# A gated mix of a state-space scan and an FFN: first loads by DMA transposes, and another order of the products

## The chip, the cores and the metric

The kernel runs on one core of a Trainium2 chip. The metric is the device time of one execution in microseconds. Before the change it is 143.59 us, the median of three runs (142.94 to 143.62).

A core has five engines with a queue of instructions each: TensorE (PE, matmuls; PEld is its weight load), VectorE (DVE), ScalarE (ACT), GpSimd (POOL) and SyncE (SP, which here only issues DMAs). Each works through its own queue in order. They wait for each other by semaphores.

## The reference

```python
x = A_x                                               # 2048 tokens x 448
g = sigmoid((x * gate_w).sum(-1, keepdims=True))
# A: a diagonal complex state-space layer, 448 states
Lam_bar = exp(exp(log_dt) * Lam)                      # Lam = Lambda_re + i Lambda_im
Bu = x @ (((Lam_bar - 1) / Lam)[:, None] * Bmat).T    # complex
h[t] = Lam_bar * h[t-1] + Bu[t]
a = 2 * real(h @ Cmat.T) + x * Dskip
# B: a dense FFN, 448 -> 1792 -> 448
b = silu(x @ w1) @ w2
out = g * a + (1 - g) * b
```

Inputs and output are bfloat16.

## The kernel before

**Products.** The 2048 tokens are worked in four chunks of 512 (`CH`). For each chunk there are seven tiles of Bu (`bu(tc, s)`: 448 real and 448 imaginary states, as 7 x 128) and fourteen tiles of the first FFN layer (`f1(tc, fb)`). Both are products over the 448 features with the transposed x (`xT`). 448 is three and a half times 128, so two tiles are always made together as a pair, on the upper and lower 64 rows of PE at once. `step` (L605) opens a pair with eight matmuls of 64 rows and closes the pair before it with six (`half_steps`, L596; `close`, L621). All of these matmuls have line L599. `BU(tc, (a, b))` and `F1(tc, (a, b))` write out such pairs. The second layer is `ffn2(tb)` (`F2`, L697): fourteen matmuls (L703) for 128 tokens. The readout of the states is `readout(tb)` (`C`, L717): seven matmuls (L731) for 128 tokens, and then VectorE's combination with the gate and x (L721, L735) and the store.

**Results and their banks.** The products land in eight banks of PSUM; a pair takes two. A bank is used again when its result has been taken out: an FFN tile by ScalarE with SiLU (L692, into `aT`), a Bu tile by ScalarE (L633) or, for four tiles of the first chunk, by VectorE (L631), into `U`. There is one `U` for all chunks, so a tile of the next chunk can be written there only after `lanes` of the chunk before has read it. A second-layer block leaves by ScalarE (L707, into `Tb`).

**The recurrence.** `lanes(tc)` (L654) turns `U` by cosines and sines (L652: products into `PA` and `PB`, and their sum), so that the complex recurrence becomes seven real scans (L665, into `Gf`). Each scan's result is converted to bfloat16 (`Gb`) by ScalarE (L671) or by GpSimd (L669); the table `GP` (L626) says which ones go to GpSimd. Then `Gb` is turned back into `H` (L652). Slot 3 is half real and half imaginary, and its halves are exchanged by two small DMAs (`swapped`).

**Parameters.** The four vectors come by ScalarE's DMA queue, are transposed by PE (L487, L489) and copied into `pc` (L495). From `pc` follow the cosine and sine tables on VectorE, ScalarE and GpSimd (L501 to L548), then `s8` and `c8` (L557, L559), and from these a chain of about twenty GpSimd operations on a few columns (`pt`, L562 and L565 to L589) to `SS`, `CC`, `sc1` and `sc2`. `readout_weights(k)` (L741) scales the transposed C with `sc2` on ScalarE (L757, L759, into `ct`) and with `sc1` on VectorE (L761, L764, into `CP`).

**Loads.** SP issues, in this order: x's first chunk as it is (`xnat`), B in four loads, w1 in ten, w2, x's second chunk by transposing DMAs (`load_xt`, L370), C by two transposing DMAs (L389) and three small loads. PE transposes x's first chunk (`x_transposes`, L437) and all of B (`b_transposes`, L459), and VectorE and ScalarE copy them out (L447, L449, L475, L477). `idle(n)` (L420) lets PE multiply zeros, n times 256 columns (L425).

**What sets the order.** `Plan` (L47) is a list scheduler that runs on the host when the program is built. PE's order is the order in which the code adds the products, written out at L800 to L868. On the other engines it picks, of the instructions that could start first by the plan's own costs, the one with the lowest `prio`. A cost is written at each instruction (0.10 to 0.15 us for the small GpSimd operations, `act_cost` and `dve_cost` for the rest). The result is a fixed order for each queue, with fixed waits.

Of the kernel before, what the change touches and what calls it, by code (L numbers as in the profile page):

```python
# [8 lines left out]
AF = mybir.ActivationFunctionType  # L9
# [252 lines left out]
def bass_gated_mix__ssm_conv_s5__dense_activation_silu__prompt_kernel(nc, A_x, A_Lambda_re, A_Lambda_im, A_B_re, A_B_im, A_C_re, A_C_im,  # L262
               A_log_dt, A_Dskip, B_x, B_w1, B_w2, gate_w, out):
    with ExitStack() as ctx:
# [24 lines left out]
        Bnat = Tb[:, 0:7, :]  # L289
# [67 lines left out]


# [7 lines left out]
        def load_xt(tc, n, prio, cost, reads=()):  # L366

            rows = slice(tc * CH, (tc + n) * CH)
            for k, (o, c) in enumerate(((slice(0, 3), slice(0, 384)), (slice(3, 4), slice(320, 448)))):
                P.add("sp", lambda e, o=o, c=c: e.dma_start_transpose(xT[:, o, rows], x2[rows, c]), list(reads),  # L370
                      [f"xT{t}{k}" for t in range(tc, tc + n)], cost[k], prio + k, sem(), n * CH * (1100, 500)[k])

        load_x(0, 0)
        load("sp", Bnat[:, 0:3, :], A_B_re[0:384, :].rearrange("(s p) d -> p s d", p=128), "Bn0", 384 * 896, 1)
        load("sp", Bnat[:, 4:7, :], A_B_im[0:384, :].rearrange("(s p) d -> p s d", p=128), "Bn3", 384 * 896, 2)
        load("sp", Bnat[0:64, 3, :], A_B_re[384:448, :], "Bn1", 64 * 896, 3)
        load("sp", Bnat[64:128, 3, :], A_B_im[384:448, :], "Bn2", 64 * 896, 4)
        for h, (c0, c1) in enumerate(((0, 384), (384, 896))):
            w = w1s[:, :, :].rearrange("p b (q f) -> p b q f", q=2)
            for b in range(3):  # L380
                load("sp", w[:, b, :, c0:c1], B_w1[128 * b:128 * b + 128, :].rearrange("p (q f) -> p q f", q=2)[:, :, c0:c1],
                     f"w1{h}{b}", 128 * 4 * (c1 - c0), 5 + h)
            load("sp", w[64:128, 3, :, c0:c1], B_w1[384:448, :].rearrange("p (q f) -> p q f", q=2)[:, :, c0:c1],
                 f"w1{h}3", 64 * 4 * (c1 - c0), 5 + h)
            load("sp", w1s[0:64, 3, c0:c1], B_w1[320:384, c0:c1], f"w1{h}4", 64 * 2 * (c1 - c0), 5 + h)
# [11 lines left out]
        def late_loads():  # L397
            load_xt(2, 2, 16, (6.0, 1.4), ["Gb7a", "Gb7b"])
            load("sp", dsk[:, :],
                 A_Dskip.rearrange("(o n) -> o n", o=1).partition_broadcast(128).rearrange("p o n -> p (o n)"),  # L400
                 "dsk", 128 * 896, 18, ["Gb7b"])
            for tc in range(1, NCH):
                load_x(tc, 18 + tc, ["Gb7b"])
# [11 lines left out]
        ACT(lambda e: e.preload_act_table(AF.Exp), [], ["tbl"], 1.3, 4)  # L415


        DVE(lambda e: e.memset(PB[:, 0, :], 0.0), [], ["PB0"], 0.2, 0)  # L418
# [10 lines left out]
        idle(15)  # L429


        def x_transposes(h, n):

            tk = Ps()

            def mm(pe):
                for q in range(2):  # L437
                    for b in range(2):
                        o = (q * 2 + b) * 128
                        c = XCOL[2 * n + q]  # L440
                        r = pe.transpose(bk16(tk)[:, o:o + 128], xnat[:, 2 * h + b, c:c + 128], ident[:, :])  # L441
                return r
            P.add("pe", mm, ["xn0", "ident"], [tk], 0.24)
            dst = xT[:, 2 * n:2 * n + 2, 256 * h:256 * h + 256]
            src = lambda: bk16(tk)[:, 0:512].rearrange("p (q n) -> p q n", q=2)
            if n == 0:
                DVE(lambda e: e.tensor_copy(dst, src()), [tk], [f"xT00{h}"], 0.42, 0)  # L447
            else:
                ACT(lambda e: e.activation(dst, src(), AF.Copy), [tk], [f"xT01{h}"], act_cost(512), 0)  # L449

        for h in range(2):
            for n in range(2):
                x_transposes(h, n)

        def xr(tc):
            return [f"xT{tc}{k}" for k in (range(2) if tc else ("00", "01", "10", "11"))]

        def b_transposes(slots, reads, h, to_act):

            tk = Ps()  # L460
            n = len(slots)

            def mm(pe):
                for q in range(2):
                    i = 2 * h + q
                    for j, s in enumerate(slots):
                        o = (q * n + j) * 128
                        r = pe.transpose(bk16(tk)[:, o:o + 128], Bnat[:, s, XCOL[i]:XCOL[i] + 128], ident[:, :])  # L468
                return r
            P.add("pe", mm, reads + ["ident"], [tk], 0.06 * 2 * n)  # L470
            dst = BT[:, 2 * h:2 * h + 2, slots[0] * 128:(slots[-1] + 1) * 128]
            src = lambda: bk16(tk)[:, 0:2 * n * 128].rearrange("p (q m) -> p q m", q=2)
            name = f"BT{h}_{slots[0]}"
            if to_act:
                ACT(lambda e: e.activation(dst, src(), AF.Copy), [tk], [name], act_cost(256 * n), 0)  # L475
            else:
                DVE(lambda e: e.tensor_copy(dst, src()), [tk], [name], 0.1 + 0.00058 * 256 * n, 0)  # L477

        B01, B23, B456 = (0, 1), (2, 3), (4, 5, 6)
        b01, b23, b456 = ([f"BT{h}_{s}" for h in range(2)] for s in (0, 2, 4))  # L480
# [11 lines left out]
        b_transposes(B01, ["Bn0"], 0, False)  # L492
        b_transposes(B01, ["Bn0"], 1, True)
        idle(2)
# [96 lines left out]

        def half_steps(pe, a, b, lo, hi, start):  # L596
            for i in range(len(lo)):
                for p0, (w, xc, tk, c0), k in ((0, a, lo[i]), (64, b, hi[i])):
                    r = pe.matmul(bk(tk), w[p0:p0 + 64, k, c0:c0 + 128], xT[p0:p0 + 64, k, xc:xc + CH],  # L599
                                  start=(start and i == 0), stop=(not start and i == 2))  # L600
            return r

        open_pair = []

        def step(ta, tb):  # L605

            (wa, xa, ca, ra, ea), (wb, xb, cb, rb, eb) = ta, tb
            a, b = Ps("pair"), Ps("pair")
            begin = lambda pe: half_steps(pe, (wa, xa, a, ca), (wb, xb, b, cb), (0, 1, 2, 3), (0, 1, 2, 3), True)
            end = lambda pe: half_steps(pe, (wb, xb, b, cb), (wa, xa, a, ca), (0, 1, 2), (0, 1, 3), False)  # L610
            reads = ra + rb

            def evict(a, b):
                ea(a)
                eb(b)
            P.add("pe", begin, reads, [a, b], 0.866, rows=64)
            if open_pair:
                close()
            open_pair.append((end, reads, a, b, evict))

        def close():  # L621
            end0, reads0, a0, b0, evict0 = open_pair.pop()
            P.add("pe", end0, reads0, [], 0.65, acc=[a0, b0], rows=64)
            evict0(a0, b0)

        GP = ((), (0, 1), (0, 1), ())  # L626


        def u_out(s, tk, on_dve=False):
            if on_dve:  # L630
                DVE(lambda e: e.tensor_copy(U[:, s, :], bk(tk)), [tk], [f"U{s}"], dve_cost(512), 2)  # L631
            else:
                ACT(lambda e: e.activation(U[:, s, :], bk(tk), AF.Copy), [tk], [f"U{s}"], act_cost(512), 4)  # L633

        def bu(tc, s):
            def evict(tk):
                u_out(s, tk, tc == 0 and s in (1, 2, 5, 6))
                if s == 3 and tc:
                    swapped(U, "U", 0)
                elif s == 3:  # L640
                    for k, p in ((0, 0), (1, 64)):
                        DVE(lambda e, p=p: e.tensor_copy(U[p:p + 64, 7, :], U[64 - p:128 - p, 3, :]),
                            ["U3"], [f"U7{'ab'[k]}"], dve_cost(512, 4), 2)
            return BT, CH * tc, 128 * s, xr(tc) + (b01, b01, b23, b23, b456, b456, b456)[s], evict

        def swapped(t, tn, prio):
            for k, (p, q) in enumerate(((0, 64), (64, 0))):
                P.add("sp", lambda e, p=p, q=q: e.dma_start(t[p:p + 64, 7, :], t[q:q + 64, 3, :]),
                      [f"{tn}3"], [f"{tn}7{'ab'[k]}"], 0.55, prio, sem(), 65536)
# [4 lines left out]
        def lanes(tc):  # L654
# [7 lines left out]
            for s in (3, 0, 4, 1, 5, 2, 6):  # L662
# [7 lines left out]
                else:  # L670
                    ACT(lambda e, s=s: e.activation(Gb[:, s, :], Gf[:, s, :], AF.Copy), [f"Gf{s}"], [f"Gb{s}"], act_cost(512), 4)  # L671
# [18 lines left out]
        def f1(tc, fb):  # L690
# [3 lines left out]
            part = 0 if fb % 7 < 3 else 1  # L694
            return w1s, CH * tc, 128 * fb, xr(tc) + [f"w1{part}{n}" for n in range(5)], evict

        def ffn2(tb):  # L697
# [3 lines left out]
            def mm(pe, tk=tk):  # L701
# [6 lines left out]
                [tk, f"g1_{tc}"], [f"Tb{tb}"] + [f"{'B' if tb < 7 else 'C'}n{k}" for k in range(4 if tb < 7 else 5)], act_cost(448, 1), 3)  # L708
# [195 lines left out]
```

## Time and profile before

| | us |
|---|---|
| median of three runs | 143.59 |
| the profiled execution | 143.92 |
| its span, first to last instruction | 142.0 |
| PE busy | 137.6 |
| VectorE busy | 126.1 |
| ScalarE busy | 79.1 |
| GpSimd busy | 34.2 |
| first-layer and Bu matmuls (L599), share of the chain that ended last | 45% |
| second-layer matmuls (L703), share of it | 30% |
| readout matmuls (L731), share of it | 15% |

The profile's page gives busy times of one execution. The chain that ended last follows the work back from the last instruction, at each step to what released it. Its pieces are listed as start, duration, engine, tile and line, with the number of instructions. A time line gives start, duration, engine, line, operation, what is written and read, and in brackets the idle time of the engine before it with what ended it. A wait is listed as who waited, for whom, and then us in total, times, and the longest.

### The profile page before, as it was taken

Reading aid. Unit: us, or ns where it says so; the run is one execution under the profiler, and the core shown is the slowest. Engines: PE = TensorE matmul, PEld = TensorE weight load, DVE = VectorE, ACT = ScalarE, POOL = GpSimd, SP = SyncE. Lnnn points to the kernel's source line nnn. Section 1 sums busy time; section 2 is a strip of 40 time slices with the busy share of each in tenths; the row PEclk is TensorE's granted clock in tenths of the full one; section 3 lists DMA queues with packets and bytes.
Section 4 is the critical chain, followed back from the end, with each engine's and each line's share of the span. In section 5 each row is a group of like instructions: output and inputs, shape, how many; then the busy total and the mean of one; then the engine's idle time right before and its main releaser. Section 6 shows DMA issues by size and latency. Waiting matters only on the chain.

```text
span 142.0 us, 2706 instructions
## 1 busy us (share of the span) xinstructions
PE 137.6 (97%) x1069; PEld 70.6 (50%) x1069; DVE 126.1 (89%) x145; ACT 79.1 (56%) x148; POOL 34.2 (24%) x66
## 2 busy tenths in 40 slices
PE   6989999999999999999999999999999999999993
PEld 4855555544444544444555554444455555555552
DVE  0399999998899299999999999999999999899393
ACT  3386698798965494889811014898721355411100
POOL 7184000089009520443450002542000000000000
PEclk9999999999999999999999999999999999999999
DMA  4989969201947600101000102000001021000113
GB/s 133 331 258 290 314 133 201 33 0 39 239 103 188 229 5 0 37 0 42 2 31 1 41 29 69 18 18 5 0 30 34 0 69 37 31 1 32 32 65 99
DMA packets 21108, 11.44 MB, mean 81 GB/s; under 512 B 11492, under 2 KB 21096, under 8 KB 21096
## 3 DMA queue, kind: packets, MB, share of 16 engines
q1 hardware_dynamic: 21088, 11.27, 30.5%
q8 instruction: 8, 0.13, 0.4%
q14 instruction: 4, 0.03, 0.1%
q10 hardware_dynamic: 8, 0.00, 0.0%
HBM read 6.25 MB, written 1.84 MB: 57 GB/s over the span
## 4 chain that ended last, share of the span: by engine, by line
PE 96%; DVE 1%; ACT 1%; POOL 1%; issue 0%
PE ps L599 45%; PE ps L703 30%; PE ps L731 15%; PE ps L425 2%; PE ps L441 1%; PE ps L774 1%; ACT BT L475 1%; PE ps L468 1%; POOL cw L562 0%; DVE ot L735 0%; PE ps L751 0%; DVE PB L418 0%; POOL gwc L497 0%; DVE pc L495 0%; DVE cw L570 0%
## 5 line engine op out<-in xcount | busy, mean ns | idle before, releaser
L599 PE MATMUL ps<-xT,w1s 64*128 64x512 bf16 x392 | 47.4, 376 | 0.0
L703 PE MATMUL ps<-w2s,aT 128*128 128x448 bf16 x224 | 44.7, 352 | 0.0
L692 ACT ACTIVATE aT<-ps 128x512 bf16<-128x512 f32 x56 | 30.0, 601 | 5.3 <-PE ps L599 5.2
L599 PEld LDWEIGHTS ps<-xT,w1s 64*128 64x128 bf16 x392 | 21.0, 94 | 22.7 <-issue 0.7
L703 PEld LDWEIGHTS ps<-w2s,aT 128*128 128x128 bf16 x224 | 21.7, 98 | 20.3 <-issue 0.4
L665 DVE TENSOR_TENSOR_SCAN Gf<-rc,gin,PA 128x512 f32<-128x512 f32 x21 | 26.8, 1322 | 0.0
L599 PE MATMUL ps<-xT,BT 64*128 64x512 bf16 x196 | 25.9, 376 | 0.7 <-DVE ph L511 0.6
L707 ACT ACTIVATE Tb<-ps,g 128x448 bf16<-128x448 f32 x16 | 10.1, 633 | 28.0 <-PE ps L703 21.4
L731 PE MATMUL ps<-CP,H 128*128 128x448 bf16 (+1 forms) x119 | 23.2, 341 | 0.0
L671 ACT ACTIVATE Gb<-Gf 128x512 bf16<-128x512 f32 x24 | 14.7, 630 | 8.4 <-DVE Gf L665 8.3
L599 PEld LDWEIGHTS ps<-xT,BT 64*128 64x128 bf16 x196 | 10.7, 94 | 12.1 <-DVE phk L508 0.8
L731 PEld LDWEIGHTS ps<-CP,H 128*128 128x128 bf16 x119 | 11.5, 98 | 9.8 <-issue 0.4
L633 ACT ACTIVATE U<-ps 128x512 bf16<-128x512 f32 x24 | 13.3, 592 | 2.2 <-PE ps L599 2.2
L735 DVE SCALAR_TENSOR_TENSOR ot<-ps,g,tf 128x448 bf16<-128x448 f32 (+1 forms) x17 | 11.1, 650 | 3.2 <-issue 2.2
L669 POOL CAST Gb<-Gf 128x512 bf16<-128x512 f32 x4 | 6.1, 1518 | 23.0 <-DVE Gf L665 23.0
L721 DVE SCALAR_TENSOR_TENSOR tf<-xnat,g,Tb 128x448 f32<-128x448 bf16 x16 | 10.6, 674 | 0.1
L652 DVE TENSOR_TENSOR PB<-Gb,SIN 128x1536 bf16<-128x1536 bf16 (+1 forms) x8 | 8.6, 1087 | 1.2 <-ACT Gb L671 1.1
L652 DVE TENSOR_TENSOR PB<-U,SIN 128x2048 bf16<-128x2048 bf16 (+1 forms) x8 | 8.6, 1080 | 0.0
L652 DVE TENSOR_TENSOR PA<-U,COS 128x3584 bf16<-128x3584 bf16 x4 | 8.1, 2020 | 0.2
L652 DVE TENSOR_TENSOR PA<-PA,PB 128x3584 bf16<-128x3584 bf16 x4 | 8.1, 2018 | 0.0
L652 DVE TENSOR_TENSOR H<-PA,PB 128x3584 bf16<-128x3584 bf16 x4 | 8.1, 2014 | 0.0
L652 DVE TENSOR_TENSOR PA<-Gb,COS 128x3584 bf16<-128x3584 bf16 x4 | 8.1, 2014 | 0.0
(97 smaller groups left out, 100.5 us busy)
## 6 DMA issues: line engine op xcount, KB each, us to landing
xnat<-in_A_x_dram SPq DMA_DIRECT2D x4, 448.0 KB, 6.1
out_dram<-ot SPq DMA_DIRECT2D x15, 112.0 KB, 1.7
w2s<-in_B_w_dram SPq DMA_DIRECT2D x1, 1568.0 KB, 9.3
w1s<-in_B_w_dram SPq DMA_DIRECT2D x3, 256.0 KB, 4.6
w1s<-in_B_w_dram SPq DMA_DIRECT2D x3, 192.0 KB, 4.3
Gb<-Gb SPq DMA_DIRECT2D x8, 64.0 KB, 1.9
U<-U SPq DMA_DIRECT2D x6, 64.0 KB, 2.0
Tb<-in_A_B_re_dram SPq DMA_DIRECT2D x1, 336.0 KB, 3.7
```

The costliest lines, as they stand in the source:

```text
L599: r = pe.matmul(bk(tk), w[p0:p0 + 64, k, c0:c0 + 128], xT[p0:p0 + 64, k, xc:xc + CH], start=(start and i == 0), stop=(not start and i == 2))
L633: ACT(lambda e: e.activation(U[:, s, :], bk(tk), AF.Copy), [tk], [f"U{s}"], act_cost(512), 4)
L652: return DVE(lambda e: e.tensor_tensor(o, a, b, op), r, w, dve_cost(n, 2), prio)
L665: DVE(lambda e, s=s, b=b, init=init: e.tensor_tensor_scan(Gf[:, s, :], rc[:, b:b + 1].to_broadcast([128, CH]), PA[:, s, :], init, ALU.mult ...
L669: POOL(lambda e, s=s: e.tensor_copy(Gb[:, s, :], Gf[:, s, :]), [f"Gf{s}"], [f"Gb{s}"], 0.75, 8)
L671: ACT(lambda e, s=s: e.activation(Gb[:, s, :], Gf[:, s, :], AF.Copy), [f"Gf{s}"], [f"Gb{s}"], act_cost(512), 4)
L692: ACT(lambda e: e.activation(aT[tc % 2][:, fb, :], bk(tk), AF.Silu), [tk, "tbl"], [f"aT{tc % 2}_{fb}"], act_cost(512), 3)
L703: r = pe.matmul(bk(tk)[:, 0:D_MOD], aT[tc % 2][:, fb, o:o + 128], w2s[:, fb, :], start=(fb == 0), stop=(fb == NFB - 1))
L707: ACT(lambda e, tk=tk: e.activation(Tb[:, tb, :], bk(tk)[:, 0:D_MOD], AF.Copy, scale=g1[:, tb:tb + 1]), [tk, f"g1_{tc}"], [f"Tb{tb}"] + [f ...
L721: DVE(lambda e: e.scalar_tensor_tensor(tf[tb % 2][:, :], xnat[:, tb, :], g[:, tb:tb + 1], Tb[:, tb, :], ALU.mult, ALU.add), [f"xn{tc}", f" ...
L731: r = pe.matmul(bk(tk)[:, 0:n], Ht[:, s, o:o + 128], CP[:, s, c], start=(s == 0), stop=(s == NSLOT - 1))
L735: DVE(lambda e, tk=tk, c=c, n=n: e.scalar_tensor_tensor(ot[tb % 3][:, c], bk(tk)[:, 0:n], g[:, tb:tb + 1], tf[tb % 2][:, c], ALU.mult, ALU ...
```

## The change

Six things change.

- x's first chunk comes by two transposing DMAs (as the other chunks do), B by six (`load_bt`); the transposes on PE and their copies are gone. `xnat` of the first chunk is loaded later, with the others.
- w1 comes in three parts of columns (`W1C`: 256, 256 and 384 of each half) instead of two; the first part's four loads are issued from ScalarE's queue, ahead of the parameters.
- PE multiplies zeros 44 and 4 times instead of 15 and 2. The parameter transposes stand behind the 44.
- The products have another order: FFN tiles come ahead of Bu, and most later groups are mixed anew.
- Conversions on GpSimd (`GP`): slots 0, 1, 4 in the first and second chunk and 0, 1 in the third, where there were 0, 1 in the second and third.
- Some priorities in the plan: U's eviction on ScalarE 4 to 3.5, the `Gb` conversions on ScalarE 4 to 1, `ct[0]` 2 to 3, `ct[1]` 2 to 4, `CP[k]` 5 to 3, `CP[4+k]` 5 to 21.5, the first table load 4 to 3.5.

```diff
-        load_x(0, 0)
-        load("sp", Bnat[:, 0:3, :], A_B_re[0:384, :].rearrange("(s p) d -> p s d", p=128), "Bn0", 384 * 896, 1)
...
+        load_xt(0, 1, 0, (1.45, 0.7))
+        def load_bt(name, src, rows, col, cost, prio):
+            n = rows.stop - rows.start
+            for k, (o, c) in enumerate(((slice(0, 3), slice(0, 384)), (slice(3, 4), slice(320, 448)))):
+                P.add("sp", lambda e, o=o, c=c: e.dma_start_transpose(BT[:, o, col:col + n], src[rows, c]), [],
+                      [f"{name}{k}"], cost[k], prio + 0.1 * k, sem(), n * (768, 256)[k])
+        load_bt("BTr", A_B_re, slice(0, 448), 0, (1.4, 0.7), 2)
+        load_bt("BTi", A_B_im, slice(0, 384), 512, (1.3, 0.65), 3)
+        load_bt("BTj", A_B_im, slice(384, 448), 448, (0.7, 0.6), 4)
+        def load_w1(eng, h, prio):
+            c0, c1 = W1C[h:h + 2]
...
+        load_w1("act", 0, -1)
+        load_w1("sp", 1, 5)
+        load_w1("sp", 2, 6)
...
-            for tc in range(1, NCH):
+            for tc in range(NCH):
                 load_x(tc, 18 + tc, ["Gb7b"])
...
-        idle(15)
+        idle(44)
...
-        b_transposes(B01, ["Bn0"], 0, False)
-        b_transposes(B01, ["Bn0"], 1, True)
-        idle(2)
+        idle(4)
...
-        GP = ((), (0, 1), (0, 1), ())
+        GP = ((0, 1, 4), (0, 1, 4), (0, 1), ())
...
+        F1(0, (1, 8))
         BU(0, (0, 1))
-        b_transposes(B456, ["Bn3"], 0, False)
...
+        F1(0, (0, 7))
+        close()
+        BU(0, (5, 6))
         gates(0)
-        BU(0, (4, 5), (6, 2))
-        step(bu(0, 3), f1(0, 7))
-        F1(0, (0, 8), (1, 9), (2, 10), (3, 11), (4, 12), (5, 13))
+        step(bu(0, 3), f1(0, 9))
+        F1(0, (2, 10))
+        BU(0, (2, 4))
+        F1(0, (3, 11))
         lanes(0)
+        F1(0, (4, 12), (5, 13))
+        step(f1(1, 0), bu(1, 3))
+        BU(1, (6, 2), (0, 1))
+        step(f1(0, 6), f1(1, 13))
+        F1(1, (2, 8))
         late_loads()
         skip(0)
-        step(f1(0, 6), f1(1, 13))
-        F1(1, (1, 7), (2, 8))
+        F1(1, (6, 12))
         close()
+        F1(1, (1, 7))
+        BU(1, (4, 5))
+        F1(1, (3, 9))
         F2(0)
-        step(f1(1, 0), bu(1, 3))
-        BU(1, (0, 1), (4, 5), (6, 2))
-        F1(1, (3, 9), (4, 10), (5, 11), (6, 12))
-        close()
-        gates(1)
-        readout_weights(0)
-        readout_weights(1)
-        F2(1)
-        readout_weights(2)
-        readout_weights(3)
-        F2(2, 3)
-        lanes(1)
+        readout_weights(2)
+        gates(1)
+        readout_weights(1)
+        F2(1, 3)
+        lanes(1)
+        F2(2)
+        readout_weights(3)
+        gates(2)
+        F1(2, (1, 9))
+        BU(2, (4, 5))
+        readout_weights(0)
...
-        F2(12)
-        C(8)
-        F2(13)
-        C(9)
+        C(4, 5, 6)
+        F2(10, 8)
+        C(7)
+        F2(11, 12, 9, 13)
+        C(8, 9)
         F2(14)
+        lanes(3)
         C(10)
         F2(15)
-        C(11)
-        C(12, 13, 14, 15)
+        C(11, 12, 13, 14, 15)
```

## The prediction

> **What bounds the kernel now.** I read the page's shares first, then the chain that ended last in order of time, then the list of waits, then the time lines of single engines where a wait had shown.
>
> ```profile
> PE 137.6 (97%) x1069; PEld 70.6 (50%) x1069; DVE 126.1 (89%) x145; ACT 79.1 (56%) x148; POOL 34.2 (24%) x66
> ```
>
> ```profile
> 1.18 3.38 PE ps L425 x15
> 4.56 1.71 PE ps L441 x16
> ...
> 6.59 0.19 DVE pc L495
> ...
> 7.90 1.02 PE ps L599 x8
> 8.92 0.79 PE ps L468 x12
> ...
> 10.69 18.95 PE ps L599 x174
> ...
> 139.57 0.45 DVE ot L735
> ```
>
> TensorE is the bound. From 10.69 to 139.54 the chain is PE alone, 128.85 us without a hole. With the first eight product matmuls (0.87 without their drain) and the first gates (0.54), which run inside the head, that is 130.3 us that no order of products shortens. The span of 142.0 is that, plus 2.45 after 139.54, plus 9.25 of head without products. The change can save only in the head, and can lose wherever PE is made to wait. One pair of FFN or Bu tiles is 14 matmuls: 14 x 18.95/174 = 1.52 us, 0.87 for the opening eight and 0.65 for the closing six.
>
> The waits show two that cost nothing today:
>
> ```profile
> ACT ct L757 <- POOL sc L583: 3.1, 1, 3.1
> DVE CP L761 <- ACT ct L757: 3.1, 1, 3.1
> ```
>
> ScalarE stands 3.1 us before the first readout-weight scaling (L757), because GpSimd has not finished `sc2` (L583); VectorE stands as long behind it. The time lines of GpSimd and VectorE say why:
>
> ```profile
> 28.77 0.64 POOL L586 COPY SS<-s 128x3 f32<-128x3 f32 x1 [16.47 <-ACT s L557]
> 29.38 1.16 POOL L562 TENSOR_TENSOR cw<-rc,s 128x4 f32<-128x4 f32 x1
> ...
> 42.79 2.03 POOL L585 COPY CC<-c 128x3 f32<-128x3 f32 x1
> 44.79 1.22 POOL L565 TENSOR_SCALAR cw<-cw 128x4 f32<-128x4 f32 x1
> ...
> 47.82 0.24 POOL L583 TENSOR_SCALAR sc<-cw 128x4 f32<-128x4 f32 x1
> ```
>
> ```profile
> 42.75 2.02 DVE L652 TENSOR_TENSOR PA<-U,COS 128x3584 bf16<-128x3584 bf16 x1
> 44.69 1.22 DVE L652 TENSOR_TENSOR PB<-U,SIN 128x2048 bf16<-128x2048 bf16 x1
> ```
>
> A GpSimd operation on a few columns takes 0.2 us when VectorE is idle, but beside a VectorE operation it ends when that one ends: 42.79+2.03 = 44.82 against 44.77, 44.79+1.22 = 46.01 against 45.91. So while VectorE is busy the chain to `sc2` moves about one link per VectorE instruction. The plan charges 0.10 to 0.15 a link. PE did not notice the 3.1 us: it was in two second-layer blocks (2.65 us each, one bank each) and needed no eviction.
>
> **The change part by part.**
>
> *Head.* Removed from PE: 16 x transposes (1.71) and 28 B transposes (0.45+1.1); from VectorE their copies (0.84+0.42+0.87), from ScalarE 1.2+0.6+1.3. Added: dummies 44+4 for 15+2. The 15 dummies are 0.211 us apart ((4.35-1.18)/15) and the 16 transposes after them 0.107; the eight transposes from 6.49 take 0.056 each. PE's rate doubled near 6.25. So 24 dummies at 0.211 fill 1.18 to 6.25, 20 at 0.107 last to 8.4, the parameter transposes (0.29) to 8.7, four dummies (0.43) to T0 = 9.15. From T0 the 130.3 + 2.45 give 141.9: against 142.0 the head is worth 0.1. The Trainium skill, "TensorE: Matmul & The Clock Gate", Part 1, puts the warm-up at about 3.4 us of activity, varying by run; this trace took 5.1. By the page 16 slow and 28 fast dummies would end at 7.6, T0 would be 8.35 and the head worth 0.9 (an estimate from the page); I keep the row, and the old head would gain by an early clock too.
>
> *Loads.* On SP eight transposing loads come first. Rows: 448 rows by 3 blocks issue in 1.33 and 1.79, 1024 by 3 in 3.08, 512 by 1 in 1.25; I take 1.5, 1.2, 1.35, 1.0, 1.2, 0.85, 0.5, 0.5 = 8.1 (the plan's own 7.5 and 9.5 as ends), so to 8.9. Landing is 3.7 to 4.4 after the issue starts when nothing is queued ahead: x at about 6.0, B's real part at 7.5 to 8.5, its imaginary part at 10 to 11.5. They are wanted at T0, T0+0.87 = 10.0 and T0+4.6 = 13.7: hidden. The far end is the 10.1 us of the transpose that queued behind w2: x at 0.73+10.1 = 10.8, a loss of 1.7. The w1 columns on ScalarE's queue (4 issues at up to 0.6, as on SP) push the four parameter loads to 3.1-4.4 and the first table load to 5.6. Parameters landing 3.5 to 4.9 later, as w1's loads did, come at 6.6 to 9.3, wanted at 8.4: 0 to 0.9; I take 0, since they are 0.9 KB each. The rest of w1 issues from 8.9 to 13.8 and lands by 13.5 and 17.5, wanted at 15.1 and 19.7: hidden. w2 (issued at 14) lands at 21.5 to 23.3, x's second chunk 2.5 behind it at 24 to 26, wanted at T0+15.2 = 24.35: 0 to 1.7 of stall, which the next part swallows. C's transposes land 3.3 behind that, 27.3 to 29.
>
> *Order and priorities: the path that sets the end.* `pc` moves from 6.59 to 8.95, as the parameter transposes now stand behind 44 dummies. From `pc` VectorE runs without a hole to the end of the first lanes sum (25.03+2.02 = 27.05), 20.5 us; less the copies of B (1.29) that is 19.2, so the sum ends at 28.1, with small waits for U 28.5. `s8` can come once ph (7 us before the sum's end, 21.2) and ScalarE's queue allow, at 22.5. Then 21 GpSimd links lie before `sc2`. Until 28.5 VectorE runs five instructions, which lets through 5 or 6. Then VectorE itself stops: its next instruction in program order is the first CP, which needs `ct0`, which needs `sc2`. Freed, the remaining 16 take 0.17 each (twelve from 45.98 to 48.06): 2.8, `sc2` at 31.3. Bounds: all links free, 14 after c8 at 25.8 x 0.17 = 28.2; the rows beside scans (6.5 us for the first seven) and then 42.30 to 48.06 for the rest, 22.7+6.5+5.8 = 35. I take 31.3, nearest to the stretch 45.98-48.06, because VectorE's stop is written in the program.
>
> In the old order ScalarE's scaling stood where PE needed no eviction. Now it stands in ScalarE's queue right after the first chunk's last FFN tile (free at 27.1), and behind it wait the evictions of f1(1,0), U3, U6, U2 of chunk 1. PE has eight banks, four pairs. Step 14 needs the pair of step 10, f1(1,0) with bu(1,3). PE reaches it at T0 + 13 x 1.52 + 0.87 + 0.54 = 30.35. ScalarE starts `ct0` at 31.35, then 0.56 for it, 0.49 for the FFN tile, 0.59 for U3: free at 33.0. PE stalls 2.65. The next step needs U6 and U2; a second scaling and the conversion of Gb3 stand between (33.0 + 0.56 + 0.49 + 0.54 + 0.59 = 35.15), PE is there at 33.0+1.52 = 34.55: 0.6 more. Sum 3.2.
>
> *Four more conversions on GpSimd* (eight instead of four; three each in the first two chunks). One takes 1.52 there and lengthens the scan beside it from 1.255 to 1.564: 0.31 x 4 = 1.2 us of VectorE. Cover: the last H. It ended at 130.1; plus 5.5 (first scan from 27.1 to 32.7), plus 1.2, less the holes of 3.1 and 1.1 that go, gives 132.6 to 134; PE wants it at 142.0+3.2-7.8 = 137.4. Hidden by 3 us; without that cover it would cost its 1.2.
>
> Sum: -0.1 + 3.2 = +3.1. Span 145.1; the profiled time of 143.92 becomes 147.0. That execution lies 0.33 above the median of the runs, 143.59; the forecast for the median is 146.7.
>
> **Rivals.**
>
> *The links are not held up* (other side). `sc2` by 28.2 and C landed by then: `ct0` at 28.7 or earlier frees U3 by 30.35 and PE never waits. The point that decides is `ct0` at 28.7. Then the head alone counts: 143.5, and 142.9 at the lower end of the runs shown (142.94 to 143.62). For it: 0.2 us links at 46 us. Against: the 1.2 and 2.0 us links, and C's landing at 27.3 to 29. 14%.
>
> *The head is late.* x's or the parameters' transfers, now all in flight together at the start, arrive after 9.15. For it: the 10.1 us transpose. Against: that one queued behind w2, and 3.4 us for the first x load, 448 KB, today. Up to 1.7 on top of the 3.2: 148.4. 16%.
>
> *The chain is longer still*: `sc2` at 33 to 35 would make the stall 5 to 7, 149 to 150. Against: VectorE stops. 4%.
>
> **How the numbers follow.** The forecast's case has 66%, own range 145.2 to 148. With the others the range is 143.4 to 148.6. About 0.5% (0.7 us) is what a measurement of this kernel tells from no change. Faster: somewhat more than half of the first rival, 9%, with a product start before 9.15. Same: the rest of it, and a stall of PE that stays under 0.7, 8%. Slower: 83%.
>
> **What would show it.** The new profile should have: the first product near 9.15; a wait of ScalarE `ct` on GpSimd `sc` of about 4 us near 27-31, with VectorE's CP behind it; PE idle 2 to 3.5 us near 30-33, ended by a ScalarE eviction, and some 0.5 us near 35; no PE hole later; scans of 1.5 us beside eight GpSimd casts. I am wrong if `sc2` is ready before 28.7, if PE's hole lies before 10 us, or if C's last blocks wait for H.

## The result, and the profile after

The changed kernel takes 152.84 us (median of four runs, 150.73 to 153.71) against 143.61 us of before beside it (142.94 to 144.21). Here and below the medians are of all runs, while the ratios leave out every run over 1.5% above the fastest of its kernel, here 153.66 and 153.71. The ratio is 1.054, 95% interval 1.043 to 1.065. The forecast was 146.7 with a range of 143.4 to 148.6. The direction was right, the size was not: +9.2 us by the median and +7.8 by the ratio, where +3.1 was forecast. Even the fastest run, 150.73, lies above the range.

The profiled execution took 153.66 us, its span is 151.1 (before: 143.92 and 142.0). In the changed kernel the products have line L458, the evictions of U L489 (ScalarE) and L487 (VectorE), those of the FFN tiles L662, the parameter transposes L514, `sc2` L609, the first scaling L727 and its CP L731, the plain loads L355 and the transposing ones L371 (x) and L379 (B). On the page, the busy times, and the clock that TensorE was granted, in tenths, in 40 slices of 3.8 us:

```profile
PE 141.2 (93%) x1056; PEld 71.4 (47%) x1056; DVE 126.4 (84%) x140; ACT 74.5 (49%) x139; POOL 39.3 (26%) x70
...
PEclk9999959999689999999999999999999999999999
```

PE does fewer instructions than before (1056 for 1069) and is busy 3.6 us longer. The clock row says why: in slice 6 and in slices 11 and 12 it falls. In before it did not fall behind the first product.

The chain that ended last (start, duration, what):

```profile
4.37 4.42 DMA prm<-in_gate_w_dram
...
17.29 0.50 ACT U L489
18.02 6.41 PE ps L458 x42
...
27.06 0.10 ACT s L583
...
36.18 0.20 POOL sc L609
...
36.49 0.67 ACT ct L727
37.16 0.48 ACT aT L662
37.64 0.50 ACT U L489
38.18 9.41 PE ps L458 x70
```

Where before had PE alone from 10.69 on, this chain runs over the parameters, VectorE and ScalarE up to 18.02, and again over ScalarE and GpSimd from 24.45 to 38.18. PE itself stands three times: for the parameters at 8, at 16 to 18, and at 35 to 38 us. The waits (total, times, longest):

```profile
PE ps L458 <- ACT U L489: 5.3, 2, 3.2
ACT ct L727 <- POOL sc L609: 4.9, 1, 4.9
...
DVE CP L731 <- ACT ct L727: 4.7, 3, 4.2
...
PE ps L514 <- DMA prm<-in_gate_w_dram: 1.2, 1, 1.2
```

And the two holes with what follows them, by stretches (length; busy time of PE, PEld, DVE, ACT, POOL with the number of instructions; then the granted clock, the share of the DMA engines and GB/s):

```profile
15.90:18.02 2.12, 0.00 (x1) 0.03 (x1) 2.12 (x4) 2.12 (x6) 0.65 (x2) 1.00 0.74 159
18.02:20.50 2.48, 2.48 (x15) 1.08 (x17) 0.23 (x1) 1.42 (x2) 0.28 (x1) 0.60 0.78 205
...
35.00:38.18 3.18, 0.00 (x0) 0.00 (x0) 0.88 (x2) 1.69 (x4) 1.31 (x8) 1.00 0.00 0
38.18:41.00 2.82, 2.82 (x18) 1.06 (x20) 2.82 (x4) 2.82 (x6) 0.10 (x1) 0.65 0.20 53
```

Behind each hole the trace's clock records show half clock for 3.41 us (18.53 to 21.94 and 39.01 to 42.42): 15 matmuls in 2.48 us where the undisturbed rate gives about 23. At half clock 3.41 us hold the work of 1.71, so each drop costs 1.7 us.

The loss, by the prediction's own count (span = start of the first product + 132.75): the first product comes at 9.85, which makes 142.6 (+0.6); the holes add 2.12 and 3.19; the two drops add 3.4. Together 151.3, against 151.1. The runs of 150.73 and 152.02 show a mean clock of 0.989 where the profiled one has 0.977: one drop fewer.

### The profile page after: what moved, and what is told of

It is laid out like the page before. It is cut to its first block, busy times and chain, and to the rows that moved or that the text cites. A ratio compares the mean times of both kernels' runs of the same rounds, so it can differ in the third digit from the quotient of the medians.

```text
span 151.1 us, 2671 instructions
## 1 busy us (share of the span) xinstructions
PE 141.2 (93%) x1056; PEld 71.4 (47%) x1056; DVE 126.4 (84%) x140; ACT 74.5 (49%) x139; POOL 39.3 (26%) x70
## 4 chain that ended last, share of the span: by engine, by line
PE 78%; POOL 6%; ACT 5%; DVE 3%; DMA 3%; ACTq 2%; issue 1%
PE ps L458 34%; PE ps L673 28%; PE ps L701 14%; POOL cw L588 4%; DMA prm<-in_gate_w_dram 3%; ACTq L355 2%; ACT aT L662 1%; DVE Gf L552 1%; ACT U L489 1%; DVE Gf L549 1%; POOL SS L613 1%; PE ps L744 1%; DVE Gf L551 1%; ACT SIN L563 1%; ACT COS L571 1%
## 5 line engine op out<-in xcount | busy, mean ns | idle before, releaser
L458 PE MATMUL ps<-xT,w1s 64*128 64x512 bf16 x392 | 51.6, 392 | 3.2 <-ACT U L489 3.2
L673 PE MATMUL ps<-w2s,aT 128*128 128x448 bf16 x224 | 43.9, 353 | 0.0
L662 ACT ACTIVATE aT<-ps 128x512 bf16<-128x512 f32 x56 | 30.9, 596 | 12.9 <-PE ps L458 12.8
L458 PEld LDWEIGHTS ps<-xT,w1s 64*128 64x128 bf16 x392 | 21.1, 97 | 28.0 <-ACT U L489 4.3
L458 PE MATMUL ps<-xT,BT 64*128 64x512 bf16 x196 | 28.8, 386 | 2.1 <-ACT U L489 2.1
L635 DVE TENSOR_TENSOR_SCAN Gf<-rc,gin,PA 128x512 f32<-128x512 f32 x21 | 26.9, 1337 | 0.0
L701 PE MATMUL ps<-CP,H 128*128 128x448 bf16 (+1 forms) x119 | 22.5, 341 | 0.0
L458 PEld LDWEIGHTS ps<-xT,BT 64*128 64x128 bf16 x196 | 11.4, 96 | 13.5 <-issue 2.9
L639 POOL CAST Gb<-Gf 128x512 bf16<-128x512 f32 x8 | 11.4, 1452 | 20.4 <-DVE Gf L635 20.4
L701 PEld LDWEIGHTS ps<-CP,H 128*128 128x128 bf16 x119 | 11.5, 98 | 9.8 <-issue 0.4
L489 ACT ACTIVATE U<-ps 128x512 bf16<-128x512 f32 x24 | 13.5, 598 | 0.8 <-PE ps L458 0.8
L641 ACT ACTIVATE Gb<-Gf 128x512 bf16<-128x512 f32 x20 | 12.3, 628 | 1.1 <-DVE Gf L635 1.1
L635 DVE TENSOR_TENSOR_SCAN Gf<-rc,PA 128x512 f32<-128x512 f32 x7 | 9.1, 1359 | 0.0
L622 DVE TENSOR_TENSOR PB<-U,SIN 128x1536 bf16<-128x1536 bf16 (+1 forms) x8 | 8.6, 1082 | 0.1
L439 PE MATMUL ps<-PB 128*128 128x256 bf16 x48 | 7.4, 328 | 1.0 <-DVE PB L432 1.0
```

Source lines behind the costliest of these rows:

```text
L622: return DVE(lambda e: e.tensor_tensor(o, a, b, op), r, w, dve_cost(n, 2), prio)
L635: DVE(lambda e, s=s, b=b, init=init: e.tensor_tensor_scan(Gf[:, s, :], rc[:, b:b + 1].to_broadcast([128, CH]), PA[:, s, :], init, ALU.mult ...
L639: POOL(lambda e, s=s: e.tensor_copy(Gb[:, s, :], Gf[:, s, :]), [f"Gf{s}"], [f"Gb{s}"], 0.75, 8)
L662: ACT(lambda e: e.activation(aT[tc % 2][:, fb, :], bk(tk), AF.Silu), [tk, "tbl"], [f"aT{tc % 2}_{fb}"], act_cost(512), 3)
L673: r = pe.matmul(bk(tk)[:, 0:D_MOD], aT[tc % 2][:, fb, o:o + 128], w2s[:, fb, :], start=(fb == 0), stop=(fb == NFB - 1))
L701: r = pe.matmul(bk(tk)[:, 0:n], Ht[:, s, o:o + 128], CP[:, s, c], start=(s == 0), stop=(s == NSLOT - 1))
```

## The experiments

All kernels were run beside before, which had medians of 143.56 to 144.06 in these sets. Edits are against the changed kernel unless another is named. Two theories stood at the beginning. A: the new loads come too late for the products that wait for them, and PE's holes bring its clock down. B, the prediction's: the new order puts ScalarE's scalings, which wait for `sc2`, ahead of evictions that PE needs. C, in the expectations, is the part of A about the clock.

### Loads alone, order alone

**loads_only**: the loads of after, with the order of products, the priorities and the conversions of before.

```diff
-        F1(0, (1, 8))
         BU(0, (0, 1))
...
-        GP = ((0, 1, 4), (0, 1, 4), (0, 1), ())
+        GP = ((), (0, 1), (0, 1), ())
```

> The new loads (x and B by transposing DMAs, w1 in three parts, 44 + 4 dummies) with the order of products, the priorities and the GpSimd conversions of before. Theory A (SP's queue is late): SP still issues its eight transposes until 12.0 us, so B's imaginary part lands at 10.9 to 13.1 and x's second chunk at about 28, and PE, which wants the latter at about 25, stands 2 to 4 us there; each hole followed by 1.7 us of half clock. 146.5 to 150 us. Rival (the order of products does it all): no hole over 1 us, 143 to 144.5 us.

149.98 us, ratio 1.042 (1.034 to 1.050). The new loads cost some 6 us with the old order too; the theory that only the order hurts falls. In the profiled execution (373.5 us) every matmul was slow from start to end, which nothing here explains.

**loads_only_b**, the same kernel, for its profile:

> The loads of after with the order, priorities and conversions of before, as in loads_only, whose profiled execution was a disturbed one. Theory A (the new loads arrive too late for any order): the first product near 9.8, TensorE holes of 2 to 5 us in sum that lie where a part of B, w1 or x lands late, one or two stretches of 3.4 us at a clock of 0.5 behind them, span 146.5 to 148.5. Theory B (only the new order makes holes): no hole after the first product, span 142.7.

147.72 (profiled, span 145.7) and 150.17, the second with a clock of 0.988. TensorE's time line, the instructions that it stood idle before:

```profile
9.24 0.21 PE L514 MATMUL ps<-ident,prm 4*128 4x4 bf16 x3 [1.35 <-DMA prm<-in_gate_w_dram]
16.56 1.24 PE L458 MATMUL ps<-xT,w1s 64*128 64x512 bf16 x9 [0.34 <-ACT U L489]
...
28.05 1.26 PE L458 MATMUL ps<-xT,w1s 64*128 64x512 bf16 x10 [1.65 <-issue]
```

The first product comes at 10.05 (+0.8 by the count above), holes of 0.34, 0.31 and 1.65 follow. The largest ends when x's second chunk lands (28.0, issued behind w2). So there are three late loads, not one: the parameters, w1's later parts, x's second chunk. Which of them shows depends on the order.

**order_only** (against before): the order, priorities and conversions of after with before's loads; B's later transposes behind the first Bu pair.

```diff
+        F1(0, (1, 8))
         BU(0, (0, 1))
...
-        GP = ((), (0, 1), (0, 1), ())
+        GP = ((0, 1, 4), (0, 1, 4), (0, 1), ())
```

> The loads of before (x and B transposed on PE) with the new order of products, priorities and GpSimd conversions; B's second and third transposes stand behind the first Bu pair. Theory B (the scaling of C stands in ScalarE's queue before GpSimd has finished sc2): ScalarE waits for GpSimd 3 to 5 us near 28 to 35, PE stands 2 to 3.5 us behind it, then half clock for 3.4 us: 147 to 151 us, with a later start of the products (w1's first part lands at 9.6). Rival (only SP's queue matters): no wait of ScalarE on GpSimd over 1 us, 144 to 145 us.

147.14 us, 1.027 (1.020 to 1.035), span 145.3, and not as expected: there is no wait of ScalarE for GpSimd and no hole near 30. `sc2` is ready at 25.1, since `pc` is there at 6.8 and not at 9.6. All of the loss lies at the start, where the new order wants w1 first (it lands at 9.8):

```profile
9.90 1.85 PE L599 MATMUL ps<-xT,w1s 64*128 64x512 bf16 x8 [2.54 <-DMA w1s<-in_B_w_dram]
```

```profile
9.90:13.40 3.50, 3.50 (x18) 1.60 (x20) 3.50 (x7) 1.26 (x2) 1.87 (x2) 0.51 0.94 255
```

A hole of 2.54 and again 3.41 us at half clock: 145.3 - 2.54 - 1.7 = 141.1, below before's 142.0. By this subtraction the new order by itself is no slower; no run shows it without the hole. The hole at 35 of after needs both, the order that puts the scalings in front and the parameters that come late.

### The two holes and the clock

**w1_on_act**: w1's second part is issued from ScalarE's queue, behind the parameters, and not from SP's behind the transposing loads.

```diff
+        some = named("w110", "w111", "w112", "w113")
+        for o in some:
+            o.eng = "act"
+        move(some, named("prm3")[0])
```

> The changed kernel, every queue as it is, but w1's second part is issued from ScalarE's queue behind the parameters. Theory A: the hole of 2.1 us at 16 us was the wait for that part, though the profile names ScalarE's eviction of U; it lands before 12 us now and the hole goes, but ScalarE's wait for GpSimd moves forward by no more than 3 us: 149 to 150.5 us. Rival (the hole is ended by the eviction of U at 17.8, as the profile has it): the hole stays at 1.5 to 2.1 us, 151.5 to 153 us.

149.18 us, 1.040 (1.034 to 1.046), span 146.5. The hole at 16 is gone. The profile of after names a ScalarE eviction as what ended it, at 17.8. That eviction is even later here (17.32 to 17.92), and PE goes on at 16.09 all the same. It was w1's second part, whose last two loads land in after at 17.5 and 17.7. The hole of the scalings is still there, earlier, and in this execution no drop follows:

```profile
31.84:34.57 2.73, 0.00 (x1) 0.01 (x2) 0.89 (x2) 1.70 (x4) 0.92 (x6) 1.00 0.00 0
34.60:37.50 2.90, 2.45 (x22) 0.97 (x24) 2.90 (x4) 2.90 (x6) 0.22 (x1) 1.00 0.23 60
```

This trace has no clock records, so its 1.00 alone says nothing; that the matmuls behind the hole start in pairs 0.216 us apart, where after at half clock has 0.427, says that the clock was full. The other three runs of this kernel have a mean clock of 0.987 or 0.988, one drop each.

SP's time line in after says why the part is late (start, duration):

```profile
0.72 2.83 SPq L371 DMA_TRANSPOSE xT<-in_A_x_dram  x2
3.60 3.20 SPq L379 DMA_TRANSPOSE BT<-in_A_B_re_dram  x2
6.84 5.16 SPq L379 DMA_TRANSPOSE BT<-in_A_B_im_dram  x4
12.04 5.89 SPq L355 DMA_DIRECT2D w1s<-in_B_w_dram  x8
```

Eight transposing loads hold SP's queue until 12.0, where the forecast had 8.9. Each takes 1.23 to 1.9 us, the narrow ones too (64 rows: 1.24 and 1.23), while w1's plain loads behind them take 0.47 to 0.68 but for one of 1.50. Everything behind them comes 3.1 us late.

**ct_late**: the first two scalings on ScalarE and their CPs on VectorE stand behind the last conversion of the first chunk.

```diff
+        move(named("ct0")[0:1] + named("CP2") + named("ct0")[1:2] + named("CP1"), named("Gb6")[0])
```

> The changed kernel, every queue as it is, but the first two scalings of C on ScalarE and VectorE are moved behind the first chunk's last conversion. Theory B with C (a hole costs itself and then 1.7 us of half clock): the hole of 3.2 us at 35 us goes, and with it one drop of the clock, 4.5 to 5 us less than the changed kernel: 147 to 148.5 us. Rival (PE waits there for U, because the first lanes are late whatever ScalarE does): the hole stays over 2 us, 151 to 153 us.

149.82 us, 1.035 (1.028 to 1.043). The hole of the scalings is gone, as the theory has it. But PE now comes to x's second chunk before it is there (it lands at 29.7), a wait that the hole had covered. The hole at 16 (1.88 here) is followed by no drop of the clock, this one is:

```profile
26.88:29.79 2.91, 0.00 (x1) 0.03 (x1) 2.88 (x3) 1.27 (x3) 2.91 (x3) 1.00 0.94 177
29.84:33.25 3.41, 3.41 (x18) 1.45 (x20) 3.38 (x3) 0.26 (x1) 3.32 (x4) 0.50 1.02 188
```

**fill12**: 18 matmuls of 256 columns in front of the pair that waits at 16 us, and 28 in front of the pair ahead of the one that waits at 35, so that PE does not idle.

```diff
+        for n, k in ((18, 4), (28, 13)):
+            if n:
+                fill(n, begins[k])
```

> The changed kernel, every queue as it is, with 18 more dummy matmuls (1.9 us) before the pair that waits at 16 us and 28 (3.0 us) before the pair ahead of the one that waits at 35 us. What the two holes wait for is untouched. Theory C (a hole of 2 to 3 us costs itself and then 1.7 us, because the granted clock falls to half for 3.4 us): the holes shrink below 0.5 us, the granted clock stays at 1.0 in all runs, 149 to 150.3 us with a spread under 1 us. Rival (the matmuls after a hole are slow for another reason, DMA traffic or their first weight loads): 152 to 153.5 us and slow matmuls at the same places.

151.39 us, 1.054 (1.049 to 1.060); span 148.6, with no drop in the clock records (the other three runs give 1.0 too). The same stretches as in after:

```profile
18.02:20.50 2.48, 2.48 (x25) 1.09 (x25) 1.18 (x3) 1.85 (x3) 0.71 (x2) 1.00 0.85 211
...
38.18:41.00 2.82, 2.72 (x26) 1.08 (x24) 2.82 (x4) 2.82 (x7) 1.56 (x2) 1.00 0.29 75
```

25 matmuls where after did 15. So the idle of PE is what brings the clock down, and busy work in its place keeps it. The span falls by 2.5 and not by 3.4; 0.43 of the difference is the first product, which came at 10.28 here, the rest I do not attribute. Against the two runs of after with one drop (spans 148.7 and 149.7) fill12 gains nothing (148.6 to 149.8), and the ratio is the same 1.054. So fill12 shows what brings the clock down, but not the price of a drop. The 1.7 rests on the matmul counts, and on runs of one kernel that differ by one drop: b_mix took 146.89 and 147.24 us at a mean clock of 0.988 and 145.62 to 145.94 at 0.999 or 1.0, w1a_ctl_xt 148.50 at 0.988 and 146.44 to 146.84 at 1.0.

**gp_old**: the conversions as in before.

```diff
-        GP = ((0, 1, 4), (0, 1, 4), (0, 1), ())
+        GP = ((), (0, 1), (0, 1), ())
```

> The changed kernel with the GpSimd conversions of before (slots 0 and 1 of the second and third chunk alone); the planner lays the queues anew around that. If the conversions are hidden, as the forecast says, the time is that of the changed kernel, 151 to 153.5 us, with VectorE's scans of the first chunk at 8.4 us in all where they were 9.5. Rival (they cost on the path): 1 us less or more, under 150.5 us.

151.5 us, 1.052 (1.046 to 1.058), with the same two holes. The seven scans of the first chunk take 8.4 us in sum for 9.5, but the span is 151.1 as in after: hidden, as forecast.

### Mending it

**w1a_ctl_xt**: both edits together (w1's second part on ScalarE's queue, scalings late) and x's second chunk ahead of w2.

```diff
+        move(named("xT10", "xT11"), named("w123")[0])
```

> The changed kernel with three moves in its queues and nothing else: w1's second part on ScalarE's queue behind the parameters, x's second chunk on SP ahead of w2, the first two scalings of C behind the first chunk's last conversion. If the late loads and the scaling explain the loss: no hole over 0.7 us after the first product at 9.9, the span is that plus 130.3 and 2.5, 142.7 to 143.7, and the time 144.5 to 145.5 us. Rival (there is a further cost in the order itself or in the conversions on GpSimd): a new hole before 65 us, or PE waiting for H at the end, 146 to 148 us.

146.73 us, 1.024 (1.016 to 1.031), span 144.4, no drop of the clock in the profile (one run of four, 148.50 us, has one). One hole of PE is left behind the first product, 1.73 at 54, and it is mine:

```profile
PE ps L458 <- DVE CP L731: 1.7, 1, 1.7
```

The CP that reads the last transposed C out of its bank now comes too late.

**w1a_ctl_xt_cp3**: as that, and this CP ahead of two products of the second chunk on VectorE.

> As w1a_ctl_xt, and CP3 ahead of the two PB products of the second chunk on VectorE, so that the bank with the transposed C is read about 2 us earlier. If the 9.1 us of span that after lost are the head (0.7), two holes with their clock drops and the masked wait for x, and nothing else, this kernel has no hole of TensorE over 0.3 us after the first product at 9.85, a clock of 1.0 throughout and a span of 142.5 to 143 (before: 142.0); time 144.5 to 145. If there is a further loss in the new order itself (more work for TensorE or VectorE, conversions), the span stays above 143.5.

147.25 us, 1.024 (1.020 to 1.028), span 144.8, clock 1.0. A miss: that hole is gone, and three others come at 60 to 68 us, 1.76 in sum, before tiles that wait for an eviction:

```profile
PE ps L458 <- ACT U L489: 1.5, 2, 0.8
```

The U evictions wait for the recurrence of the chunk before. VectorE's chain starts from the parameters 2.8 us later than in before (9.5 for 6.8), and the first H is ready at 49.8 for 42.6; with PE's early holes closed, VectorE's lateness is what PE meets next. Late parameters alone are not the reason: in order_only they come as early as in before (6.8), and the first H is ready at 49.5. What makes it late in the new order was not isolated. So the count above (0.6 + holes + drops) is right for after and not for what it would be without the holes: about 2 us more were covered.

**w1a_ctl_xt_prm**: as w1a_ctl_xt, with the parameters ahead of w1's first part, and w1's second part behind the first.

```diff
+        move(named("w100", "w101", "w102", "w103"), named("prm3")[0])
```

> As the run before, and the four parameter loads are issued ahead of w1's first part on ScalarE's queue. If they were late because of w1 ahead of them: PE's wait of 1.2 us for the parameters at 8 us goes, the first product starts at 8.9 to 9.3, pc 0.7 us earlier: 0.6 us less than the run before, 143.8 to 145 us, and level with the kernel before (143.8). Rival (w1's first part then lands after 9.3 and takes its place): no gain.

149.9 us, 1.043 (1.039 to 1.048). The parameters come sooner (PE takes them at 8.09 without a wait), and then PE waits for w1's first part, which they were put ahead of, and for B's real part:

```profile
10.51 1.04 PE L458 MATMUL ps<-xT,w1s 64*128 64x512 bf16 x8 [1.53 <-DMA w1s<-in_B_w_dram]
12.77 1.47 PE L458 MATMUL ps<-xT,BT 64*128 64x512 bf16 x6 [1.22 <-DMA BT<-in_A_B_re_dram]
```

Here two holes of 1.5 and 1.2 us, one microsecond apart, were enough for the clock to fall (12.28 to 15.69).

### Is there something in the idea?

The transposes of B on PE are real work, 28 x 0.056 = 1.6 us. Four kernels, all made from before, take only that part.

**b_dma**: x as in before, all of B by DMA transposes, w1's first part from ScalarE's queue behind the parameters, x's second chunk ahead of w2; one mixed and one FFN pair ahead of the second pair of Bu alone, the scalings behind the first H, and 15 and 6 dummies.

```diff
-        b_transposes(B01, ["Bn0"], 0, False)
-        b_transposes(B01, ["Bn0"], 1, True)
...
+        load_bt("BTr", A_B_re, slice(0, 448), 0, (1.4, 1.4), 1)
+        load_bt("BTi", A_B_im, slice(0, 384), 512, (1.3, 1.3), 2)
+        load_bt("BTj", A_B_im, slice(384, 448), 448, (1.25, 1.25), 3)
...
+        load_w1("act", 0, 4.5)
```

> Before with only B by DMA transposes (x's first chunk as it was, transposed by TensorE), w1 in three parts with the first one issued from ScalarE's queue behind the parameters and the table load, x's second chunk ahead of w2, and two FFN pairs ahead of the second Bu pair. TensorE loses 28 transposes (1.55 us at full clock), of which the four of the first pair lie beside a wait. If all loads land in time: first product near 7.8, no hole over 0.3, span 140.6 to 141, time 142.2 to 142.6, some 1.0 us faster than before. If loads take each other's place at the start: B's real part lands after 7.9 or w1's first part after 9.9, a hole of 0.5 to 2, the clock at 0.5 behind it when the hole is over 2, time 142.5 to 146.

146.76 us, 1.018 (1.012 to 1.024). The loads take each other's place: B's real part, issued at 1.2 and 3.8, lands at 9.7 and 10.6, PE waits 3.37 us for it before the first product (10.75), and the clock falls at 12.02.

**b_mix**: only the rows of B that the first pair does not need come by DMA transposes, behind w1's first part; w1 all on SP, two FFN pairs ahead of the second Bu pair, and before's 15 and 2 dummies; otherwise as above.

> Before with only those rows of B by DMA transposes that the first pair of products does not need (real rows from 256 on and all imaginary ones, six loads behind w1's first part, all on SyncE's queue); x's first chunk and B's rows 0 to 255 come as in before and are transposed by TensorE; two FFN pairs stand between the first and the second Bu pair; w1 in three parts; x's second chunk ahead of w2. TensorE loses 20 transposes of 0.056 us = 1.1 us. If the loss in the other kernels comes only from loads that are late for what waits for them: the first product at 7.9 as in before, w1's first part in by 9.9, the loaded rows of B by 13.0 to 16, no hole over 0.3 us, clock 1.0, span 140.7 to 141.2, time 142.3 to 143.0, that is 0.4 to 0.9% faster than before. If transposing loads slow the loads around them: a hole of 0.5 to 2 us between 9 and 17 us or near 24 (x's second chunk) or 28 (w2), time 143.5 to 146.

145.91 us, 1.015 (1.011 to 1.019). Four of the six runs show no drop of the clock; the profiled one, 147.24, has one. The first product comes early (6.86 in the profiled execution, where PE was granted full clock from 3.97), then:

```profile
18.21 0.58 PE L613 MATMUL ps<-xT,BT 64*128 64x512 bf16 x1 [3.69 <-ACT U L647]
```

Again the profile names ScalarE. The program's waits of that pair are w1's second part too, which SP issues behind six transposing loads, from 13.26, and which lands at 18.1.

**b_mix_act** (against b_mix): those four loads from ScalarE's queue, behind its second table load.

```diff
+        some = named("w110", "w111", "w112", "w113")
+        for o in some:
+            o.eng = "act"
+        move(some, [o for o in named("dtc") if "tbl" in o.writes][0])
```

> b_mix with the four loads of w1's second part issued from ScalarE's queue behind its second table load (from about 8.2 us on) and not from SyncE's behind the six transposing loads. If b_mix's hole (14.5 to 18.2) was the issue time of the transposing loads on SyncE's queue ahead of w1's second part: that part lands by 13 to 14.5, the hole goes or shrinks under 0.5, the clock stays at 1.0, w1's third part may leave up to 1 us near 17; span 139.7 to 141, time 141.3 to 142.8, that is 1 to 2% faster than before. If the loads are slowed by each other, whichever queue issues them: w1's second part lands at 16 or later, a hole of 1.5 us or more near 14.5, time 144 to 146.

143.34 us against 143.60, ratio 0.9975 (0.9953 to 0.9997), twelve runs, clock 1.0. The hole is gone: issued from 8.15 on, the part lands at 11.1 to 13.5. It was the place in the queue, and not transfers that slow each other. What is left is 0.67 us at 17.34:

```profile
18.01 1.25 PE L613 MATMUL ps<-xT,w1s 64*128 64x512 bf16 x9 [0.67 <-DVE U L645]
```

The expected 1 to 2% did not come: the first product was at 8.16 (7.88 in before), and 0.67 went into the hole. That is faster than before by 0.25%, inside the 0.5% that a measurement of this kernel tells from no change.

**b_mix_u5** (against b_mix_act): VectorE's eviction of U5 one instruction earlier.

```diff
+        seq.remove(u5)
+        seq.insert(seq.index(abs1), u5)
```

> b_mix_act with VectorE's eviction of U5 ahead of the second absolute value of the trigonometric argument (1.2 us) instead of behind it. In b_mix_act the hole of 0.67 us at 17.34 ended with the end of that eviction (17.27 to 17.96), behind two such operations (15.00 to 17.35). If the hole is that queue: the eviction ends near 16.9, the hole is 0.1 or less (w1's third part lands at 18.97 and is then wanted at 18.85), span 140.9 to 141.0 at the same start of products, time about 142.7 against 143.34. If the bank was not free for another reason, the hole stays and the time with it.

143.7 us against 143.63, ratio 1.0009 (0.9985 to 1.0033). No gain. In this execution the first product came at 7.16, a microsecond sooner, and PE then stood 1.10 us for B's transposing loads (the last one but two landed at 14.3) and still 0.61 for an eviction. The start moves by a microsecond between executions with the moment at which the full clock is granted, and the loads do not move with it. In these four kernels that leaves of the idea no more than can just be measured.

## Why the prediction was wrong, point by point

*What bounds the kernel.* PE alone from the first product on: right, and so the loss could be added up from PE's holes.

*Head, -0.1.* It came to +0.6. The parameters were given 0 to 0.9 and I took 0; they cost a wait of 1.17 (7.87 to 9.04), issued from 3.08 behind w1's four loads and in by 8.79. I had argued that they are small. Their size did not matter, the place in the queue did: in w1a_ctl_xt_prm, first in the queue, they cost no wait. With this hole before 10 us one of the prediction's own signs of being wrong came true.

*Loads, "hidden".* This is the step that failed first. "The rest of w1 issues from 8.9 to 13.8" rested on 8.1 us for eight transposing loads, with 0.5 for the narrow ones. They took 11.3, none under 1.23. w1's second part landed at 17.7, wanted at 15.9: a hole of 2.12 that I had priced at nothing. The transposing loads themselves landed later than forecast too (x's second at 7.9 for about 6.0, B's last at 13.1 for 11.5), but PE waited for none of them. The nearest row had been there, 1.25 for 512 rows by one block, and I scaled it down by the size. The Trainium skill, "Advanced Engine Details and Errata", section "X-Bar Transpose (TRN2)", says that transposing DMAs are as fast as plain ones. For the landing b_mix agrees: the six transposing loads of B land 2.4 to 4.5 us after the start of their issue, w1's loads around them 2.8 to 4.4. At the start of after x's two take 5.8, w1's four beside them 2.9 to 5.2; no run compares equal bytes. The time that they hold the issuing queue is another matter: in b_mix 1.23 to 1.95 against 0.46 to 0.67.

*The stall for x's second chunk, "which the next part swallows".* Right in kind: it landed at 28.0, just in time. ct_late uncovered it at 2.91.

*The chain to `sc2`.* The mechanism was right. ScalarE waited 4.91 for it (forecast about 4.3), VectorE's CP 4.19 behind it, and PE 3.19 (forecast 2.65 + 0.6). That the stall itself fits is partly luck: `sc2` came at 36.4 and not 31.3, and PE came late too. `s8` came at 26.9 (forecast 22.5), the lanes sum ended at 33.1 (28.5), and from there the chain took 3.3 (2.8). VectorE had lost time in the first hole, standing for tiles of U that PE had not made:

```profile
20.77 1.29 DVE L487 CAST U<-ps 128x512 bf16<-128x512 f32 x2 [2.52 <-PE ps L458]
...
31.09 2.02 DVE L622 TENSOR_TENSOR PA<-PA,PB 128x3584 bf16<-128x3584 bf16 x1
```

```profile
36.14 0.23 POOL L609 TENSOR_SCALAR sc<-cw 128x4 f32<-128x4 f32 x1
```

order_only shows that the order hurts only together with a late `pc`. The prediction had both in its sum, and the first rival's deciding point (`ct0` at 28.7) lay where an early `pc` would have put it (order_only's starts at 27.65).

*The clock.* The second step that failed: the sum had no term for it. It cost 3.4 of the 9.1 us of span in the profiled execution. The prediction itself showed that PE's rate doubles some time after the start, and never asked what a hole of 2.6 us would do to it. The Trainium skill, "TensorE: Matmul & The Clock Gate", Part 1, describes a free-running window of 3.41 us and the half clock after an idle window. The length agrees: each drop lasted 3.41, and the edges of the records lie whole multiples of it apart (in after full clock from 4.88 to 18.53 is four, from 21.94 to 39.01 five). Less idle than a window was enough here: eight holes of 2.09 to 3.69 us, in six kernels, each brought a drop; 2.73 in w1_on_act brought none, nor did 1.65, 1.73 and 1.88.

Which hole brings a drop comes out of the traces when PE's idle time is added up in stretches of 3.41 us laid at these edges. Twelve traces have clock records. The nine stretches ahead of a drop hold 2.05 to 3.09 us of idle; no other stretch from the first product on that ends before the last matmul holds more than 1.73. Some of them:

| stretch | idle of PE | clock in the next |
|---|---|---|
| gp_old 14.58 to 17.99 | 2.05 | 0.5 |
| after 15.12 to 18.53 | 2.12 | 0.5 |
| w1a_ctl_xt_prm 8.86 to 12.28 (two holes) | 2.27 | 0.5 |
| after 35.60 to 39.01 | 2.58 | 0.5 |
| ct_late 16.18 to 19.60 (most of the hole of 1.88) | 1.45 | 1.0 |
| w1a_ctl_xt_prm 56.65 to 60.06 | 1.73 | 1.0 |

So a hole that an edge cuts in two can pass without a drop. An estimate puts w1_on_act's there: its matmuls double their rate at 5.3, eight stretches later is 32.6, and the hole from 31.84 to 34.57 is cut into 0.77 and 1.96. Where the edges lie differs between executions (full clock began at 4.88 in after and 4.34 in gp_old), so one kernel can have one drop or two.

*Conversions, hidden.* Right (gp_old).

*Rivals.* "The head is late" happened in part (the parameters) but gave 0.6 and not 1.7. That w1's later parts would hold PE up was in no case, so the range could not reach: it had the head and the stall for `sc2`, and neither this hole (2.12) nor the clock (3.4).

What stays open is where between 1.73 and 2.05 us of idle the limit lies (with the estimate for w1_on_act, above 1.96); no run placed a hole on purpose.

## What to carry to other kernels

Before a load is called hidden, add up the issue time of everything ahead of it in its queue, and price transposing loads of this size (up to 512 rows) by their count more than by their size. A hole in TensorE costs its length, and some 1.7 us more for the clock when about two microseconds of idle fall into one stretch of 3.41; several late loads cover each other, so that mending one uncovers the next, and only the sum of all tells what a version is worth. Where a wait's named releaser is an eviction that ended just then, look at what else the program waits for at that place.

## What the runs showed of the hardware that was not expected

- A transposing load on SP's queue holds it 1.23 us at the least, also for 64 rows by 128 columns; 448 or 512 rows by three blocks took 1.39 to 1.89 in after. Behind the load of w2 (1568 KB) one held it 5.9 us in after and 7.5 in ct_late.
- TensorE was granted half its clock for one stretch of 3.41 us after each of the nine stretches with 2.05 us of idle or more, and after none with 1.73 or less (in b_mix the drop began before the hole's end, at 17.6); dummy matmuls in the holes' place kept the clock at 1.0.
- The full clock at the start was granted between 3.97 and 7.08 us in kernels with the same first instructions, which moves the first product by over a microsecond (6.86, 7.16 and 8.16 in the b_mix family).
